# Unit 3's keys and values ahead of the last quarter of W2, and new early orders on four engines

## The chip, the core and the metric

The kernel runs on one core of one Trainium2 chip. Its engines are TensorE (PE, matmuls; PEld is its weight load), VectorE (DVE), ScalarE (ACT), GpSimd (POOL) and SyncE (SP). They work from instruction streams of their own and wait for one another on semaphores. The metric is the device time of one execution in microseconds, as the median of several runs. The kernel before takes 292.14 us (three runs, 292.03 to 292.19).

## What is computed

A linear attention with softmaxes over q's features and over k's sequence, then a feed-forward layer with an ELU:

```python
q_s = softmax(q, axis=-1)                    # 8 batches, 8 heads, 576 tokens, 64 features
k_s = softmax(k, axis=2)                     # over the 576 tokens
kv  = einsum('bhsd,bhse->bhde', k_s, v)
x   = einsum('bhsd,bhde->bhse', q_s, kv)     # -> 4608 tokens x 512
h   = x @ w_in                               # 512 -> 2048
g   = where(h > 0, h, exp(min(h, 0)) - 1)
out = g @ w_out                              # 2048 -> 512
```

## The kernel before, in words

**Units and blocks.** The attention runs in 16 *units*, four heads of one batch each (two units per batch). For unit n, `stage1` takes the exponentials of q and k on ScalarE, casts v to bf16 (tile `VB`), reduces q over features and takes the reciprocal on VectorE (`ZQ`, `RZQ`), and multiplies (`QS`) on VectorE or GpSimd. `tp` transposes `QS` on TensorE and copies it into `qsT`; from unit 4 on a transposing DMA on SyncE's queue (`turn`, tile `QT`) and a widening copy (`widen`) do it. `kv_mm` forms k^T v in PSUM, `m` divides by k's sums into `MBLK`, `ao_mm` (or `ao_parts` for units 0 and 1) multiplies `MBLK` with `qsT` into attention tokens, and `xt` copies them into the ring `XT`. A unit's nine chunks of tokens come in two pieces, so `ao` and `xt` run twice.

The feed-forward part runs in 9 *blocks* of 512 tokens. In each, 8 *groups* g of 256 columns of W1 are multiplied with `XT` (`hg_mm`, four steps kc over the 512 features, two column tiles: 8 matmuls, line 620), then the ELU follows in `hg` (exponential at line 646, relu at 648, and a GR step at 652 or 659, that writes `GR` from PSUM and so empties two banks). Blocks 0 and 1 multiply `GR` with W2 in `out_mm` (line 673, 512 columns, four matmuls for a quarter of W2). Blocks 2 to 8 use a form with fewer products on sums of GR and of W2's quarters (`pair`, line 806).

**PSUM.** Eight banks in four pairs: b0 and b1, b2 and b3 (called `D_`), b4 and b5 (`C`), b6 and b7 (`AB`). In blocks 0 and 1 the pairs are shared between groups, W2 accumulators (one bank for each of four token tiles, `ts`) and the units' small products. Units from 2 on use `AB`, and unit 3 uses `C` for its transpose and its first token piece.

**Loads.** SyncE issues q, k and v of units 0 and 1 in the first 4 us. GpSimd issues W1, first in four pieces of 384 KB (groups 0 to 2, one piece for each kc, the kc=0 piece only when k of unit 0 has landed), then groups 3, 4 and 5 singly (512 KB each) and 6 with 7 (1 MB), then W2 in four quarters of 1 MB (`load_w2`, resources `W2_0` to `W2_3`) mixed with the loads of units 2 and 3 (576 KB each). A transfer's landing is what its readers wait for.

**What sets the order.** The whole program is a list of about 1400 operations, each added with `Sched.add`, with the resources that it reads (R), writes (W) or holds (X). Dependencies follow from the order in which operations are added. The order on each engine is written out by hand in `ORDER`, as numbers in that list; where an operation may run on either of two engines (copies on ScalarE or VectorE, multiplies and casts on GpSimd, VectorE or ScalarE), its place in `ORDER` says which. `AFTER` adds four extra dependencies. Before unit 1's k^T v step (`spare_until`), spare matmuls fill TensorE's gaps as `Sched.fill` reckons them.

Block 0's order on TensorE: the small products of units 0 and 1; groups 0 to 2, kc by kc; groups 3, 4, 5, 7, 6; then the 16 steps of `out_mm` over four quarters of W2 (`jq`) and four token tiles, with the small products of units 2 and 3 between them; then block 1's groups.

## Time and profile before

| | |
|---|---|
| median of three runs | 292.14 us |
| span of the profiled execution | 290.4 us |
| TensorE busy | 280.6 us (97%) |
| VectorE busy | 225.5 us (78%) |
| ScalarE busy | 209.7 us (72%) |
| GpSimd busy | 167.8 us (58%) |
| TensorE's share of the chain that ended last | 94% |
| granted TensorE clock | 0.999 |
| moved by DMA | 50.04 MB, 172 GB/s over the span |

The page gives no time of the profiled execution other than its span, which runs from the first to the last instruction; the 1.7 us between it and the median lie around the span. Busy time of an engine counts its instructions without waits. A row of waits reads: who waited, for what, total us, number of times, longest. A row of the chain or of the timeline reads: start in us, length in us, engine, line, operation, tiles, count. A row of DMA issues ends with the size and the us from issue to landing. In the fences of the prediction, rows of one engine at one place come from the timeline of that stretch.

### The profile page before, as it was taken

The numbers are of one execution on the slowest core, as the hardware profiler recorded it, in microseconds if no ns is written. First come the engines' busy times: TensorE is split into PE (matmuls) and PEld (weight loads), VectorE is DVE, ScalarE is ACT, GpSimd is POOL, SyncE is SP. The second block draws the span as 40 slices with busy tenths as digits, with TensorE's granted clock in tenths as the row PEclk, the third lists the DMA queues.
The fourth block names the chain that finished last, engine by engine and source line by source line (L and its number), as shares of the span: only waits on it lengthen the run. The fifth ranks groups of instructions, "written<-read, shape, count | busy, mean of one in ns | idle before, by whom it ended". The sixth has DMA issues, their size and how long they took to land.

```text
span 290.4 us, 5465 instructions
## 1 busy us (share of the span) xinstructions
PE 280.6 (97%) x2176; PEld 243.7 (84%) x2176; DVE 225.5 (78%) x425; ACT 209.7 (72%) x237; POOL 167.8 (58%) x161
## 2 busy tenths in 40 slices
PE   2899999999999999999999999999999999999995
PEld 0488787778888899989999988989999999988995
DVE  3758834777699978989996987688977786794884
ACT  4857839989899899968995598975385656665510
POOL 1991335523869778676574886757314234277741
PEclk9999999999999999999999999999999999999999
DMA  7999999798896838739939295313102002300334
GB/s 259 399 363 390 389 389 339 163 260 323 238 349 163 241 91 228 202 78 305 178 96 222 56 292 129 76 40 71 46 18 56 0 2 67 78 2 1 92 73 128
DMA packets 36474, 50.04 MB, mean 172 GB/s; under 512 B 16352, under 2 KB 18144, under 8 KB 36448
## 3 DMA queue, kind: packets, MB, share of 16 engines
q1 hardware_dynamic: 29680, 33.96, 43.7%
q0 software_dynamic: 6528, 15.47, 17.8%
q8 instruction: 17, 0.28, 0.5%
q10 hardware_dynamic: 240, 0.26, 0.3%
q14 instruction: 9, 0.07, 0.1%
HBM read 36.70 MB, written 9.44 MB: 159 GB/s over the span
## 4 chain that ended last, share of the span: by engine, by line
PE 94%; DMA 2%; POOL 2%; SPq 0%; issue 0%; DVE 0%
PE PS L620 46%; PE PS L806 32%; PE PS L673 10%; PE PS L538 3%; DMA KR<-in_k_dram 2%; PE PS L507 2%; POOL W L377 1%; POOL VB L277 0%; PE PS L457 0%; POOL QS L433 0%; SPq L359 0%; PE PS L550 0%; DVE OSB L815 0%
## 5 line engine op out<-in xcount | busy, mean ns | idle before, releaser
L620 PE MATMUL PS<-XT,W 128*128 128x512 f32 x576 | 142.0, 393 | 0.1
L620 PEld LDWEIGHTS PS<-XT,W 128*128 128x128 f32 x576 | 105.0, 188 | 21.2 <-DVE GR L659 0.5
L652 DVE SCALAR_TENSOR_TENSOR GR<-PS,GE 128x512 fp32r<-128x512 f32 x112 | 76.8, 686 | 18.7 <-ACT GE L648 16.7
L646 ACT ACTIVATE GE<-PS 128x1024 f32<-128x1024 f32 x56 | 57.4, 1025 | 40.0 <-PE PS L620 34.2
L757 POOL TENSOR_TENSOR GR<-GR 128x256 fp32r<-128x256 f32 (+1 forms) x48 | 47.2, 996 | 31.5 <-DVE SB L757 16.6
L648 ACT ACTIVATE GE<-GE 128x1024 f32<-128x1024 f32 x56 | 59.4, 1061 | 1.4
L806 PE MATMUL PS<-W,GR 128*128 128x256 f32 x336 | 53.7, 283 | 0.0
L806 PE MATMUL PS<-TB,GR 128*128 128x256 f32 x336 | 51.3, 283 | 0.0
L806 PEld LDWEIGHTS PS<-W,GR 128*128 128x128 f32 x336 | 47.6, 191 | 1.7
L806 PEld LDWEIGHTS PS<-TB,GR 128*128 128x128 f32 x336 | 45.7, 191 | 0.7
L433 POOL TENSOR_TENSOR QS<-QR,RZQ 128x1152 f16<-128x1152 f32 (+1 forms) x16 | 30.4, 1898 | 21.4 <-DVE RZQ L423 19.7
L815 DVE TENSOR_TENSOR OSB<-OSB,PS 128x256 f32<-128x256 f32 x84 | 34.7, 416 | 10.3 <-PE PS L806 9.2
L673 PE MATMUL PS<-W,GR 128*128 128x512 f32 x128 | 32.7, 396 | 0.0
L757 POOL TENSOR_TENSOR GR<-SB,GR 128x256 fp32r<-128x256 f32 (+1 forms) x18 | 17.3, 971 | 24.6 <-PE PS L806 12.7
L673 PEld LDWEIGHTS PS<-W,GR 128*128 128x128 f32 x128 | 23.3, 188 | 5.0 <-DMA W<-in_moe_w_out_dram 0.5
L757 POOL TENSOR_TENSOR SB<-GR 128x256 fp32r<-128x256 f32 (+1 forms) x20 | 19.2, 965 | 13.7 <-DVE GR L652 6.4
L421 DVE TENSOR_REDUCE ZQ<-QR 128x18 f32<-128x1152 f32 (+2 forms) x18 | 21.7, 1207 | 6.1 <-ACT QR L419 4.8
L757 DVE TENSOR_TENSOR GR<-GR 128x256 fp32r<-128x256 f32 (+1 forms) x36 | 21.3, 603 | 0.6 <-PE PS L806 0.6
L277 POOL CAST VB<-VR 128x1152 bf16<-128x1152 f32 (+1 forms) x11 | 11.9, 1084 | 13.1 <-DMA VR<-in_v_dram 13.1
L646 ACT ACTIVATE ESB<-PS 128x1024 f32<-128x1024 f32 x16 | 16.1, 1024 | 4.5 <-PE PS L620 3.4
L399 ACT ACTIVATE KR<-KR 128x1152 bf16<-128x1152 f32 x16 | 18.4, 1155 | 0.8 <-DMA KR<-in_k_dram 0.8
L277 ACT ACTIVATE XT<-PS 128x512 fp32r<-128x512 f32 (+6 forms) x23 | 13.6, 595 | 6.3 <-PE PS L538 3.2
(58 smaller groups left out, 271.4 us busy)
## 6 DMA issues: line engine op xcount, KB each, us to landing
out_dram<-OSB SPq DMA_DIRECT2D x61, 128.0 KB, 2.4
QR<-in_q_dram SPq DMA_DIRECT2D x12, 576.0 KB, 4.9
KR<-in_k_dram SPq DMA_DIRECT2D x12, 576.0 KB, 6.3
VR<-in_v_dram SPq DMA_DIRECT2D x12, 576.0 KB, 5.1
W<-in_moe_w_out_dram POOLq DMA_DIRECT2D x4, 1024.0 KB, 16.7
QR<-in_q_dram POOLq DMA_DIRECT2D x4, 576.0 KB, 12.1
VR<-in_v_dram POOLq DMA_DIRECT2D x4, 576.0 KB, 13.0
KR<-in_k_dram POOLq DMA_DIRECT2D x4, 576.0 KB, 11.1
```

What stands on the lines that cost most here:

```text
L277: return e.activation(dst, src, AF.Copy) if e is self.nc.scalar else e.tensor_copy(dst, src)
L399: S.add("act", t_act(1152, False), lambda e: e.activation(ek[:, :, :, :].rearrange("p h c d -> p (h c d)"), flat(k), AF.Exp), key - 2, X=[ ...
L421: S.add("dve", t_dve(m), lambda e, qp=qp, zp=zp: e.tensor_reduce(zp, qp, AX.X, ALU.add), key - 3, R=[f"qR{i}{x}" for x in xs], W=[f"ZQ{i}{ ...
L433: lambda e, qp=q[:, :, a:b, :], rz=rz, dst=qs[:, :, a:b, :]: e.tensor_tensor(dst, qp, rz, ALU.mult),
L620: last = e.matmul(P[:, t * 512:(t + 1) * 512], self.W1[:, kc, tt * 128:(tt + 1) * 128], self.XT[:, kc, rc:rc + BLK], start=(kc == 0), stop ...
L646: S.add("act", t_act(1024, True), lambda e: e.activation(ge, P, AF.Exp), key, W=own, X=banks)
L648: S.add("act", t_act(1024, False), lambda e: e.activation(ge, ge, AF.Relu, bias=1.0, scale=-1.0), key, X=own)
L652: S.add("dve", t_dve(512 if j else 1024), lambda e, u=u: e.scalar_tensor_tensor(*(x[:, :, u, :] if j else x for x in (gt, P)), 0.0, ge[:, ...
L673: last = e.matmul(dst, self.tile(jb, jj, ts), self.W2[:, jj, c0:c1], start=(jj == 0), stop=(jj == 15))
L757: lambda e: e.tensor_tensor(dst, a, b, op), key, R=R, W=W, X=X, after=after)
L806: last = e.matmul(dst, a[i][:, y_, :], b[i][:, y_, :], start=start and i == 0 and y_ == 0, stop=stop and i == len(grps) - 1 and y_ == z - ...
L815: S.add("dve", t_dve(256), lambda e: e.tensor_tensor(dst, a, b, ALU.add), key, R=R, W=W, X=X, after=after)
```

## The change

The loads. W1's groups 4 and 5 come in one transfer of 1 MB. W2's last quarter comes in two halves of 512 KB, added after k and v of unit 3 in place of before them. W2's resources are named by eighths, `W2_0` to `W2_7`, and block 0's `out_mm` steps of the last quarter (`jq == 3`) are added as two steps of two matmuls each. The list has four operations more by it (one load less, one more, four steps more), so nearly every number in `ORDER` and `AFTER` is shifted by four; the `AFTER` pairs are the same operations as before.

The banks. Unit 3's transpose and its first token piece use `AB` (b6 and b7) in place of `C`.

The spare matmuls. `spare_until` is set one line earlier and names the same operation.

The orders. Up to about operation 300, that is in the first 60 us, the orders on TensorE, ScalarE, VectorE and GpSimd are new; after that they are the old ones. SyncE's is the old one throughout. With the old numbers turned into words, the differences are these.

- TensorE, start: transposes of unit 0 (both halves), unit 0's k^T v, its two token matmuls (bank 5, then 4), unit 1's second transpose, its k^T v, its first transpose, then groups 0 to 2. Before, unit 1's first transpose came second. Group 0 takes kc=0 and kc=1, group 2 kc=0, then unit 1's two token matmuls; before, the three groups' kc=0 came first.
- TensorE, W2 of block 0: unit 2's transpose after two steps (before: five); its k^T v after six (before: after all eight of the first two quarters); its first token piece directly before the third quarter's first step, its second one step later (before: three); unit 3's transpose one step after that, no longer beside unit 2's k^T v; unit 3's k^T v after all steps of the third quarter; its first token piece after three half steps of the last quarter, its second after three more; the last W2 step (bank 1) after block 1's group 1 and before its group 0.
- ScalarE and VectorE: to VectorE go unit 0's second `qsT` copy, unit 0's leftover token copy, unit 2's `qsT` copy, two W2 output copies, a token copy of unit 3, and the query multiplies of units 1, 2 and 3 for their second halves (from GpSimd). To ScalarE go the second cast of v of unit 1 (from GpSimd) and a token copy of unit 3. To GpSimd go the first-half multiplies of units 1 and 2 and unit 4's widening copy. Unit 1's second exponential of q comes before its first, unit 2's exponential of q before group 0's of block 0, unit 5's reciprocal (`RZQ`) after the first GR step of block 1's group 3.
- GpSimd's issues: W1's kc=1 piece, the cast of v of unit 0, the kc=0 and kc=2 pieces, q of unit 2, a multiply, the kc=3 piece, group 3, groups 4 and 5, groups 6 and 7, W2's first and second quarters, k and v of unit 2, q of unit 3, W2's third quarter, k of unit 3, a multiply, v of unit 3, the first half of the last quarter, the cast of v of unit 2, the second half. Before: the four kc pieces in order (the cast between the second and the third), group 3, a multiply and a cast, group 4, group 5, groups 6 and 7, W2's first quarter, q of unit 2, the second quarter, q of unit 3, v and k of unit 2, W2's third and last quarters, k and v of unit 3.

```diff
-    def load_w2(self, s, key, after=()):
+    def load_w2(self, jj0, jj1, key):
         w = self.w_out.rearrange("(jj p) c -> p jj c", p=128)
-        sl = slice(s * 4, (s + 1) * 4)
+        sl = slice(jj0, jj1)
         self.S.add("gp", ISSUE["gp"], lambda e: e.dma_start(self.W2[:, sl, :], w[:, sl, :]), key,
-                   W=[f"W2_{s}"], dma=f"w2{s}", nbytes=1 << 20, after=after)
+                   W=[f"W2_{s}" for s in range(jj0 // 2, jj1 // 2)], dma=f"w2{jj0}", nbytes=jj1 - jj0 << 18)
...
-        for g0, g1 in ((3, 4), (4, 5), (5, 6), (6, 8)):
+        for g0, g1 in ((3, 4), (4, 6), (6, 8)):
             self.load_w1(g0, g1, range(4), -30)
...
         self.side(0, -3, self.kv_mm(1, 0))
-        kv1 = S.ops[-1]
+        S.spare_until = S.ops[-1]
         self.m(1, 0, -12)
-        S.spare_until = S.ops[-4]
...
-        self.load_w2(0, -29)
-        self.load_w2(1, -29)
+        self.load_w2(0, 4, -29)
+        self.load_w2(4, 8, -29)
         for n, t in ((2, "k"), (2, "v"), (3, "q")):
             self.load(n, t, -28)
-        self.load_w2(2, -27)
-        self.load_w2(3, -25)
+        self.load_w2(8, 12, -27)
         for t in "kv":
             self.load(3, t, -26)
+        for jj in (12, 14):
+            self.load_w2(jj, jj + 2, -25)
...
-            ps, eng = (C if x == 0 else AB, "both") if n == 3 else (AB, "act")
+            ps, eng = AB, "both" if n == 3 else "act"
...
-                return n, lambda: self.tp(n, C if n == 3 else AB, due(n) - 4, ("act",))
+                return n, lambda: self.tp(n, AB, due(n) - 4, ("act",))
...
             for ts in range(4):
-                self.out_mm(0, ts, (ts + 2) % 4, 4 * jq, 4 * jq + 4, key)
+                for jj in range(4 * jq, 4 * jq + 4, 2 if jq == 3 else 4):
+                    self.out_mm(0, ts, (ts + 2) % 4, jj, jj + (2 if jq == 3 else 4), key)
...
-AFTER = ((208, 196), (227, 255), (234, 268), (300, 281))
+AFTER = ((212, 200), (231, 259), (238, 272), (304, 285))
```

4 lines of the change are left out of this document (2 added, 2 removed), and 138 rows, old and new, of the table ORDER.

## The prediction

> **What bounds the kernel now.** I read the page's head and its chain first, then the busy time by stage, then TensorE's waits, then the chain in order of time.
>
> ```profile
> span 290.4 us, 5465 instructions
> ```
>
> The chain that ends last is nearly all TensorE. The stage from 60 us on, where the change edits nothing, in the table of busy time by stretch (length, PE, PEld, DVE, ACT, POOL, clock, DMA share, GB/s):
>
> ```profile
> 60.00:287.10 227.10, 227.04 (x1725) 204.00 (x1723) 187.62 (x363) 165.42 (x183) 135.99 (x120) 1.00 0.49 128
> ```
>
> TensorE is busy for 227.04 of 227.10 us at full clock. So a shift of TensorE at 60 us reaches the end one to one, and the change is worth what it does to TensorE's position before that. What TensorE loses there (weight-load waits, then the chain in order of time: start, length):
>
> ```profile
> PEld PS L620 <- DVE GR L659: 0.5, 1, 0.5
> PEld PS L673 <- DMA W<-in_moe_w_out_dram: 0.5, 1, 0.5
> PEld PS L620 <- DVE GR L652: 0.5, 1, 0.5
> ```
>
> ```profile
> 31.80 3.06 PE PS L673 x12
> ...
> 42.63 3.67 PE PS L673 x16
> ...
> 54.05 2.11 PE PS L620 x8
> ...
> 58.95 3.91 PE PS L620 x16
> ...
> 64.57 1.81 PE PS L620 x8
> ```
>
> Undisturbed, 8 matmuls take 1.81 us, so 12 take 2.72 and 16 take 3.62. The pieces at 31.80, 54.05 and 58.95 are too long by 0.34, 0.30 and 0.29 (the one at 42.63 is not): W2's second quarter landing, VectorE emptying banks 2 and 3, VectorE emptying banks 0 and 1. Together 0.93 us, which is about all that better early orders could remove after the dense stream has begun. Its beginning is the other place:
>
> ```profile
> 14.20 1.66 PE L620 MATMUL PS<-XT,W 128*128 128x512 f32 x6
> 15.70 0.62 PE L550 MATMUL PS<-qsT,MBLK 128*128 128x512 f32 x2
> 16.16 13.32 PE L620 MATMUL PS<-XT,W 128*128 128x512 f32 x58
> ```
>
> From 14.20 us on TensorE runs at 0.227 us a matmul. Group 3 of block 0 begins 18 matmuls after 16.16, at 20.24, and group 4 at 22.06.
>
> **The change, part by part.**
>
> *W1's first pieces change places.* GpSimd now issues the piece for kc=1 first and, behind the cast of v0, the one for kc=0, which TensorE needs first. Issue times and, of single issues, us to landing:
>
> ```profile
> 8.85 0.63 POOL L377 DMA_DIRECT2D W<-in_moe_w_in_dram  x1
> ```
>
> ```profile
> W<-in_moe_w_in_dram POOLq DMA_DIRECT2D x1, 384.0 KB, 5.5
> ```
>
> The second piece lands at 8.85 + 5.5 = 14.3 whichever it is, because the queue is behind (below), and the stream can begin at about 14.36 in place of 14.20: +0.16. Could the tokens be later than that?
>
> ```profile
> 11.68 0.61 DVE L520 TENSOR_TENSOR MBLK<-PS,RZK 64x128 fp32r<-64x128 f32 x2
> ```
>
> ```profile
> 13.73 0.68 DVE L277 CAST qsT<-PS 128x512 fp32r<-128x512 f16 x1
> ```
>
> ```profile
> 12.77 0.74 ACT L277 ACTIVATE VB<-VR 128x640 bf16<-128x640 f32 x1
> 13.40 0.60 ACT L277 ACTIVATE XT<-PS 128x512 fp32r<-128x512 f32 x1
> ```
>
> Unit 0's MBLK was ready at 11.68 + 0.61 = 12.29. It no longer stands behind a reduction and two reciprocals of unit 1 on VectorE, which gains 0.5 or so. VectorE then does a query multiply (0.7, priced as the 512-wide copy) and that qsT copy (0.68) that ScalarE did, so the token matmuls start at about 13.1 (estimate), the second ends near 13.6, and ScalarE's copy (0.60) at 14.2. ScalarE also takes v1's second cast from GpSimd, but sheds two copies ahead of it; had it shed nothing, the token copy would end at 13.51 + 0.74 + 0.60 = 14.85. I take +0.16; the ends are 0 and +0.65.
>
> *Unit 2's queries ahead of W1's kc=3 piece.* 576 KB at the 388 GB/s quoted below is 1.5 us, a 384 KB piece 1.0. The pieces land at 13.3, 14.3, 15.3, the queries at 16.8, kc=3 at 17.8. TensorE first used kc=3 six matmuls after 16.16, at 17.52; it would now come at 17.68 and wait until about 17.85. So +0.33 with the first term (ends +0.1 and +0.65).
>
> *Groups 4 and 5 of W1 in one transfer.* The old three issues and the first of W2:
>
> ```profile
> 13.56 2.28 POOL L377 DMA_DIRECT2D W<-in_moe_w_in_dram  x3
> 15.83 0.76 POOL L385 DMA_DIRECT2D W<-in_moe_w_out_dram  x1
> ```
>
> ```profile
> W<-in_moe_w_in_dram POOLq DMA_DIRECT2D x1, 512.0 KB, 5.7
> ```
>
> ```profile
> W<-in_moe_w_in_dram POOLq DMA_DIRECT2D x1, 512.0 KB, 6.4
> ```
>
> ```profile
> W<-in_moe_w_in_dram POOLq DMA_DIRECT2D x1, 1024.0 KB, 9.7
> W<-in_moe_w_out_dram POOLq DMA_DIRECT2D x1, 1024.0 KB, 11.7
> ```
>
> The issues start about 0.76 apart, at 13.56, 14.4 and 15.1. Group 4 landed at 13.56 + 5.7 = 19.3, group 5 at 14.4 + 6.4 = 20.8, groups 6 and 7 at 15.1 + 9.7 = 24.8, W2's first quarter at 15.83 + 11.7 = 27.5. So the same 1 MB took 4.0 us once and 2.7 the next time. In 20.8 to 22.1 us:
>
> ```profile
> DMA packets 239, 0.50 MB, mean 388 GB/s; under 512 B 0, under 2 KB 0, under 8 KB 238
> ...
> q8 instruction: 1, 0.02, 5.5%
> ```
>
> The engines moved 388 GB/s all along, 1.55 MB in 4.0 us, so nothing was idle: one 16 KB instruction packet held up one of the 16, and the transfer landed with its slowest, 1.3 us late. [...]
> The new sequence: kc=3 at 17.8, group 3 at 19.3 (512 KB took 1.5: 20.8 against 19.3), groups 4 and 5 at 22.0, or with the packet inside their transfer at 23.3. TensorE wants group 4 at 22.06 + 0.33 = 22.4; before, it had landed 2.8 us ahead of use. Ends 0 and +0.9; I take +0.85, because the packet's old place, moved with TensorE, falls inside 19.3 to 22.0.
> [...]
>
> *The three stalls.* W2's second quarter lands about 0.3 earlier (one transfer in 2.7 in place of two in 3.0) and is used after one more step, so 0.34 goes. Block 1's groups 0, 2 and 3 now come behind one W2 step (4 matmuls, 0.9 us) put after group 1's, and VectorE frees banks 2 and 3 in time: 0.30 goes. The last (0.29) depends on ScalarE and VectorE that follow TensorE closely; I take it as gone, it may stay. Sum −0.93, ends −0.6 and −1.0.
>
> *Unit 3 in banks 6 and 7; more pieces.* All of units 2 and 3 is one row of fill, copy, fill there. The second token matmul of unit 2 now has one W2 step (0.91) before it in place of two, against 0.71 for the copy and the hops: +0.05. A transpose and a k^T v step that stood together are parted: one more restart of 0.1. Sum +0.15 (0 to +0.3). W2's last quarter in halves adds waits at two places, not matmuls.
>
> *Queues.* On GpSimd k3 and v3 pass W2's last quarter, whose first half waits behind a multiply and whose second stands behind v2's cast. By the same steps (24.8 + 1.5 − 0.3, then 2.7 for 1 MB and 1.5 for a load) the halves land at about 43.0 and 44.3, and the queue is backed up till then, so late issue costs nothing. The quarter was first used near 42.5; one more W2 step and the shift put that at 43.8 at least. If that room of 0.8 is gone, TensorE waits for what is over. SyncE's order is the same. On ScalarE the exponential of unit 2's queries now lies ahead of group 0's, in a gap it has:
>
> ```profile
> 18.18 1.94 ACT L646 ACTIVATE ESB<-PS 128x1024 f32<-128x1024 f32 x2 [1.45 <-PE PS L620]
> ```
>
> It takes about 1.2 (priced by its 1152 elements from two 1024-wide ones in 1.94), the gap is 1.45 and ends 0.33 later, so it hides; with the queries over 0.4 later than 16.8 the excess delays group 0. Copies moved to VectorE:
>
> ```profile
> 40.00:50.00 10.00, 10.00 (x82) 7.82 (x81) 2.53 (x6) 8.01 (x12) 3.39 (x4) 1.00 0.99 354
> ```
>
> VectorE is busy 2.53 of 10 us there, so some 3.5 us more hide. Finer names for W2's parts and the spare-matmul line change nothing that is run later.
>
> **Sum**: +0.33 + 0.85 − 0.93 + 0.15 = +0.4 on a span of 290.4. The median, 292.14, lies 1.7 above that span, and I keep this: about 292.5.
>
> **The rivals.**
>
> *Faster: the merged piece is in time.* If the packet falls after 22.0, or on an engine that is ahead, +0.85 goes and −0.45 is left: 291.7, with all ends favourable 291.2. For it: there are 0.4 us of room without the packet. Against it: the packet came in that place before, and the room is a third of its delay. [...]
>
> *Slower: unit 5's turned queries come late.*
>
> ```profile
> 57.72 2.12 POOL L433 TENSOR_TENSOR QS<-QR,RZQ 128x1152 f16<-128x1152 f32 x1 [1.68 <-DVE ESB L657]
> ```
>
> ```profile
> QT<-QS SPq DMA_TRANSPOSE x1, 7.5
> ```
>
> ```profile
> 67.71 1.17 ACT L277 ACTIVATE qsT<-QT 128x1152 fp32r<-128x1152 f16 x1
> ...
> 69.22 0.51 PE L538 MATMUL PS<-qsT,MBLK 128*128 128x384 f32 x2
> ```
>
> The reciprocal ahead of this multiply is moved behind the GR step of block 1's group 3. That group's matmuls end near 56.2 (54.05 + 2.11); two ScalarE passes of 1.0 and a 0.7 step on VectorE follow, with ScalarE's queue between: 59 to 60, an estimate. So the multiply starts 1.5 to 2.4 us later; with 2.4 the transpose is issued at about 62.4. It took 7.5 us before and would then land at 69.9; copy and hops end at 71.1, where TensorE wants it at 69.6: +1.6, or 294.1. It decides from 5.9 us of transpose upward. For it: this very transpose was slow, and its margin was 0.3. Against it: the 12 of the trace have a median of 4.1.
>
> ```profile
> DMA to landing us min/median/max: 2.9/4.1/7.5
> ```
>
> *Slower: VectorE's new load* reaches a bank that TensorE waits for, one multiply (0.7) late: about 293.2. Against it: the idle time above.
>
> **How the numbers follow.** Within 0.2%, 0.6 us, is about what a measurement of this kernel can tell from no change. The forecast, a stall on the merged piece against three removed stalls, 0.45: 292.5, its own range 292.0 to 292.9. In time, 0.27. Late turn, 0.20. VectorE, 0.08. Faster: two thirds of the second case, 0.18. Slower: the late turn, most of VectorE and a fifth of the forecast, 0.34. Same: 0.48. Range 291.3 to 294.0: the second case nearly whole, the late turn up to its price.
>
> **What would show it.** The first W1,XT matmul at 14.3 to 14.4; a wait near 17.8 on W1; one of 0.5 to 0.9 at 22 to 23 on W1, the largest of TensorE's after the start; no wait on W2 at 31; chain pieces of 1.81 and 3.6 at 54 and 59. Wrong if group 4 starts by 22.5, if QT lands more than 5.9 us after its issue, or if a wait on VectorE stands between 30 and 55 us.

## The result, and the profile after

The changed kernel takes 295.69 us (median of four runs, 295.51 to 296.11) against 292.08 us for the kernel before on the same chip (four runs, 292.01 to 292.19): a ratio of 1.0124 with a 95% interval of 1.0109 to 1.0138. It is 3.6 us slower. The forecast was 292.5 us, with a range that ended at 294.0.

The profiled execution's span, and the stage from 63.5 us to 290.4 us in the table of busy time by stretch (length, PE, PEld, DVE, ACT, POOL, clock, DMA share, GB/s):

```profile
span 293.7 us, 5465 instructions
```

```profile
63.50:290.40 226.90, 226.90 (x1725) 203.82 (x1723) 187.28 (x361) 165.07 (x183) 137.98 (x121) 1.00 0.48 127
```

The span grew by 3.3 us, and in the late stage TensorE is busy all the time with the same 1725 matmuls as before. The loss lies ahead of 63 us. Among the waits of TensorE's weight loads (who, for what, total, times, longest), two name the places that matter here:

```profile
PEld PS L550 <- DVE qsT L277: 2.3, 1, 2.3
...
PEld PS L620 <- DVE GR L659: 1.0, 1, 1.0
```

No wait on W1 or W2 is among the longer ones, which is where the prediction had looked. The first place in the timeline of the changed kernel (start, length, engine, line, operation, tiles):

```profile
11.84 1.44 POOL L433 TENSOR_TENSOR QS<-QR,RZQ 128x640 f16<-128x640 f32 x1
11.86 1.98 DVE L433 TENSOR_TENSOR QS<-QR,RZQ 128x512 f16<-128x512 f32 x1
13.87 0.69 DVE L277 CAST qsT<-PS 128x512 fp32r<-128x512 f16 x1
14.62 1.22 PE L550 MATMUL PS<-qsT,MBLK 128*128 128x512 f32 x2 [1.41 <-DVE qsT L277]
...
17.34 2.02 PE L620 MATMUL PS<-XT,W 128*128 128x512 f32 x6
```

Unit 1's two query multiplies start 20 ns apart, GpSimd's first. VectorE's then takes 1.98 us, ending 0.56 after GpSimd's. Behind it on VectorE stands the copy of unit 0's turned queries, for which TensorE waits. Unit 0's token matmuls start at 14.62 in place of 12.35, W1's first matmul at 17.34 in place of 14.20. The six W1 matmuls there take 2.02 us, against 1.66 before. Groups by line in that stretch (busy us, mean ns of one), for the changed kernel at 12.6 to 18.3 us:

```profile
L457 PE MATMUL PS<-ID,QS 128*128 128x128 f16 x9 | 1.4, 312 | 0.0
...
L550 PE MATMUL PS<-qsT,MBLK 128*128 128x512 f32 x2 | 1.2, 714 | 1.4 <-DVE qsT L277 1.4
```

and for the kernel before at 12.3 to 18.3 us:

```profile
L550 PE MATMUL PS<-qsT,MBLK 128*128 128x512 f32 x4 | 1.4, 421 | 0.5 <-DVE MBLK L520 0.5
...
L457 PE MATMUL PS<-ID,QS 128*128 128x128 f16 x4 | 0.4, 222 | 0.2 <-POOL QS L433 0.2
```

The same shapes take 312 ns in place of 222 and 714 in place of 421: TensorE works slowly here, until about 18.3 us. The granted clock in the table by stretch does not say so, because the trace's list of granted clocks begins only at 18.18 us in this kernel, at full rate (in the kernel before at 9.99), and the table reads 1.00 where there is no entry:

```profile
14.60:18.30 3.70, 3.68 (x50) 2.77 (x51) 2.10 (x5) 1.28 (x2) 3.70 (x6) 1.00 1.30 378
```

The second place, in the chain in order of time and then in the timeline of the changed kernel:

```profile
53.60 1.83 PE PS L620 x8
...
59.56 1.53 DVE ESB L657
...
61.11 1.23 DVE GR L659
...
62.38 3.93 PE PS L620 x16
```

```profile
59.38 1.15 POOL L277 CAST qsT<-QT 128x1152 fp32r<-128x1152 f16 x1 [0.72 <-DMA QT<-QS]
59.56 1.51 DVE L657 TENSOR_SCALAR ESB<-ESB 128x1024 f32<-128x1024 f32 x1 [1.09 <-ACT ESB L646]
```

In the kernel before, the same VectorE operation stands in the timeline so:

```profile
56.94 0.69 DVE L657 TENSOR_SCALAR ESB<-ESB 128x1024 f32<-128x1024 f32 x1 [1.09 <-ACT ESB L646]
```

Beside GpSimd's widening copy of unit 4 (which was ScalarE's before) it takes 1.51 us in place of 0.69, and block 1's group 3 (the piece of 3.93 us) waits for what follows it. The piece at 53.60 is now 1.83 us long, so the stall for banks 2 and 3 is gone as forecast. In the prediction's chain it was 2.11.

How far TensorE is behind the kernel before at the same matmul, from the starts in the traces (us; the first two rows are absolute starts). The kernels of the other columns follow below.

| matmul | before | changed | GpSimd second | copy first | mended | mended, split | widening waits | queries behind | queries ahead |
|---|---|---|---|---|---|---|---|---|---|
| first token matmul | 12.35 | 14.62 | 13.33 | 12.55 | 11.40 | 11.63 | 11.89 | 12.40 | 12.37 |
| first W1 matmul | 14.20 | 17.34 | 15.53 | 15.28 | 14.18 | 14.41 | 14.68 | 15.50 | 14.54 |
| group 3, block 0 | 20.24 | +3.50 | +1.32 | +1.07 | +1.61 | +0.64 | +1.42 | +1.40 | +0.84 |
| after block 0's groups | 29.32 | +3.50 | +1.34 | +1.07 | +1.61 | +0.79 | +1.56 | +1.44 | +0.84 |
| group 3, block 1 | 58.95 | +3.44 | +1.26 | +0.98 | +1.51 | +0.79 | +0.71 | +1.39 | +0.16 |
| unit 4's first tokens | 62.69 | +3.46 | +1.31 | +1.00 | +1.50 | +0.82 | +0.67 | +1.36 | +0.20 |
| unit 5's first tokens | 69.22 | +3.46 | +1.30 | +1.00 | +1.50 | +0.82 | +0.67 | +1.36 | +0.96 |
| block 8 | 269.43 | +3.47 | +1.31 | +0.99 | +1.59 | +0.91 | +0.76 | +1.39 | +1.08 |
| **median time** | 292.08 | 295.69 | 293.62 | 293.36 | 293.33 | 293.74 | 292.91 | 292.62 | 292.64 |

All 3.5 us are lost before 20.24 us, and what lies between 29 and 63 us, where the prediction expected a gain of 0.78 (−0.93 + 0.15), comes to −0.04. So there are two questions: what the start costs, and what ate the gain.

### The profile page after: what moved, and what is told of

Read it like the earlier page. It is cut to its first block, busy times and chain, and to the rows that moved or that the text cites. A ratio compares the mean times of both kernels' runs of the same rounds, so it can differ in the third digit from the quotient of the medians.

```text
span 293.7 us, 5465 instructions
## 1 busy us (share of the span) xinstructions
PE 282.6 (96%) x2176; PEld 245.0 (83%) x2176; DVE 231.5 (79%) x431; ACT 207.3 (71%) x232; POOL 167.9 (57%) x160
## 4 chain that ended last, share of the span: by engine, by line
PE 92%; DMA 2%; DVE 2%; ACT 2%; SPq 0%; issue 0%
PE PS L620 44%; PE PS L806 32%; PE PS L673 10%; PE PS L538 3%; DMA VR<-in_v_dram 2%; PE PS L507 2%; PE PS L457 1%; ACT ESB L646 1%; DVE QS L433 1%; ACT KR L399 1%; PE PS L550 1%; DVE ESB L657 1%; SPq L359 0%; DVE GR L659 0%; ACT VB L277 0%
## 5 line engine op out<-in xcount | busy, mean ns | idle before, releaser
L433 POOL TENSOR_TENSOR QS<-QR,RZQ 128x1152 f16<-128x1152 f32 (+2 forms) x15 | 30.1, 2006 | 21.2 <-DVE RZQ L423 18.5
L277 POOL CAST VB<-VR 128x1152 bf16<-128x1152 f32 (+1 forms) x10 | 11.0, 1096 | 11.7 <-DMA VR<-in_v_dram 11.6
## 6 DMA issues: line engine op xcount, KB each, us to landing
KR<-in_k_dram POOLq DMA_DIRECT2D x4, 576.0 KB, 10.9
```

The costliest lines, as they stand in the source:

```text
L277: return e.activation(dst, src, AF.Copy) if e is self.nc.scalar else e.tensor_copy(dst, src)
L433: lambda e, qp=q[:, :, a:b, :], rz=rz, dst=qs[:, :, a:b, :]: e.tensor_tensor(dst, qp, rz, ALU.mult),
```

## The experiments

The theory after reading the two traces: (a) the two query multiplies, put side by side by the change, hold each other up; (b) TensorE, which waits for it, works at half its speed; (c) the gain of the later orders is eaten by the widening copy on GpSimd in the same way as in (a). Rivals: the order of the copy behind the multiply alone, the transfers, the W1 pieces, ScalarE's order at 55 us. Numbers in the diffs are places in the changed kernel's list: 43 and 47 are unit 1's two query multiplies (first and second half), 35 is the copy of unit 0's turned queries, 51 the transposes of 43's product, 67 unit 2's load of queries. Each time stands beside runs of the kernel before on the same chip, whose medians were 291.9 to 292.2. Nothing of the computation is left out in any kernel but spare matmuls in one, whose results are read by nobody.

### The two multiplies

GpSimd's multiply waits for VectorE's:

```diff
-AFTER = ((212, 200), (231, 259), (238, 272), (304, 285))
+AFTER = ((212, 200), (231, 259), (238, 272), (304, 285), (43, 47))
```

> The changed kernel with one wait more: GpSimd's multiply of unit 1's first half of queries starts only when VectorE's multiply of the second half has ended. Nothing else differs. Theory (the two multiplies hold each other up, and TensorE then works on at half its speed): VectorE's multiply goes from 1.98 us back to about 0.7, the copy of unit 0's turned queries ends at about 13.3 instead of 14.57, the token matmuls start at 13.4 instead of 14.62, and the time falls by 1.2 us to about 294.4 if TensorE stays slow until 18 us as in the changed kernel, or by up to 2.7 us to 293.0 if the shorter wait lets it keep its speed. Rival (VectorE's multiply is slow for another reason, the transfers that write SBUF for one): it still takes about 2 us and the time stays at 295.7 or grows, as GpSimd's multiply now ends later.

The copy goes ahead of the multiply on VectorE:

```diff
-    "dve": ... 48 49 50 47 35 58 ...
+    "dve": ... 48 49 50 35 47 58 ...
```

> The changed kernel with two neighbours on VectorE exchanged: the copy of unit 0's turned queries goes ahead of the multiply of unit 1's second half, so the two multiplies may still meet, but the token matmuls don't wait for it. Theory: the copy runs from 11.85 to 12.55 (a copy out of PSUM isn't held up by GpSimd), token matmuls start at 12.7 instead of 14.62, and the time falls by 1.9 us to 293.8 if TensorE stays slow, or by 3 us to about 292.7 if it is fast from 12.7 on. Rival (what costs is the later queries of unit 1, not the copy behind the multiply): the multiply of the second half still ends late, unit 1's tokens with it, and the time stays within 0.5 us of 295.7.

Measured: 293.62 us (ratio to before 1.005, 1.003 to 1.007) and 293.36 us (1.0051, 1.0037 to 1.0066). Timeline of the first:

```profile
11.86 0.69 DVE L435 TENSOR_TENSOR QS<-QR,RZQ 128x512 f16<-128x512 f32 x1
...
12.63 1.26 POOL L435 TENSOR_TENSOR QS<-QR,RZQ 128x640 f16<-128x640 f32 x1 [0.66 <-DVE QS L435]
13.33 1.22 PE L552 MATMUL PS<-qsT,MBLK 128*128 128x512 f32 x2
```

and of the second:

```profile
11.80 0.69 DVE L279 CAST qsT<-PS 128x512 fp32r<-128x512 f16 x1
12.00 1.44 POOL L435 TENSOR_TENSOR QS<-QR,RZQ 128x640 f16<-128x640 f32 x1
12.53 1.47 DVE L435 TENSOR_TENSOR QS<-QR,RZQ 128x512 f16<-128x512 f32 x1
12.55 0.73 PE L552 MATMUL PS<-qsT,MBLK 128*128 128x512 f32 x2 [0.69 <-DVE qsT L279]
```

With GpSimd second, VectorE's multiply takes 0.69, and the token matmuls come 1.29 earlier, as expected; that the transfers slow it is excluded, for up to there they are the same. With the copy first, the multiplies meet again, VectorE's ends 0.56 after GpSimd's again, and a copy that reads PSUM runs beside GpSimd in 0.69. In both meetings the multiply that starts second, VectorE's, by 20 ns in the changed kernel and by 0.53 us here, is the one that grows most: 1.98 and 1.47 us against 0.69, where GpSimd's takes 1.44 against 1.26. The two kernels gained 2.1 and 2.3 us, with token matmuls that come 1.29 and 2.07 us earlier. In the first the gain is larger than that, and the rest is TensorE's speed: its token matmuls still take 1.22 us, but from 14.9 us on it is fast, in place of 18.3 (unit 1's k^T v at line 509 takes 0.49 us here, and 0.71 at 16.22 in the changed kernel):

```profile
14.85 0.49 PE L509 MATMUL PS<-VB,KR 64*64 64x65 bf16 x36
15.27 0.45 PE L459 MATMUL PS<-ID,QS 128*128 128x128 f16 x5
```

Its granted clock is first listed at 14.70 us. In the second kernel the token matmuls take 0.73: in that execution TensorE was at full rate from 9.02 us on.

### TensorE's speed after a wait

Three more spare matmuls ahead of unit 0's token matmuls (56 is the first of them) in the changed kernel:

```diff
+                count += 3 * (o.idx == 56)
                 if count > 0:
```

> The changed kernel with three more spare matmuls (on the identity, into a bank that nobody reads) ahead of unit 0's token matmuls, so that TensorE is busy through most of the 1.4 us in which it waits for VectorE there; the collision of the two multiplies stays. Theory (TensorE works at half its speed until 18 us because it was idle at 13.2 to 14.6): its matmuls are fast soon after 14.6, W1's first matmul starts at about 16.2 instead of 17.34, the whole is 1 to 1.5 us faster, 294.2 to 294.7. Rival (the slow speed lasts as long in the changed kernel whether TensorE waits or not): within 0.3 us of 295.7, or slower by what the last spare matmul takes too long (up to 0.4).

Measured: 295.79 us (1.0107, 1.0072 to 1.0142): a miss. (Two of the five executions, with a mean granted clock of 0.999 and 1.0, took 293.70 and 294.71 us; the three at 0.992 to 0.994 took 295.79 to 296.44.) The timeline of TensorE in the profiled one, of the second sort, shows why:

```profile
10.85 1.90 PE L894 MATMUL PS<-ID 128*128 128x512 f16 x8
14.80 0.73 PE L553 MATMUL PS<-qsT,MBLK 128*128 128x512 f32 x2 [2.05 <-DVE qsT L280]
...
16.18 0.71 PE L460 MATMUL PS<-ID,QS 128*128 128x128 f16 x5
```

This time TensorE had come to full speed before the spare matmuls (granted from 9.16 us on). All eight took 1.90 us and were done at 12.75, so that the wait was 2.05 and not shorter. The token matmuls (0.73) are still fast, the five transposes at 16.18 are slow, and in the table by stretch the granted clock shows it:

```profile
15.90:19.30 3.40, 3.40 (x47) 2.82 (x36) 1.38 (x5) 0.97 (x2) 3.40 (x6) 0.51 1.21 344
```

The clock falls to half for 3.4 us soon after the wait (0.51 as the mean of this stretch). In the changed kernel's own profile TensorE had not yet been fast when the wait came (its five spare matmuls at 10.90 took 2.31 us, where all eight took 1.90 here), and the slow start lasted until 18.3; the record reads 1.00 there, as it does over the first spare matmuls of the kernel before (five in 2.32 us at 5.51, four in 1.04 at 10.82). The opposite test takes spare matmuls from the kernel before, where nothing else changes:

```diff
-                if count > 0:
+                if count > 0 and free < 8500.0:
```

> The kernel before with only its first seven spare matmuls: the one at 9.6 us and the four at 10.8 to 11.9 are left out (their results are read by nobody). Theory (TensorE falls to or stays at half its speed when it waits in the start): the matmuls of units 0 and 1 and the first of W1 show durations of 0.31 us for 128x128 and 0.56 to 0.71 us for 128x512 instead of 0.22 and 0.37 to 0.45, and the time rises by 0.5 to 1.5 us. Rival (the speed doesn't hang on the spare matmuls): durations and time as before, within 0.2 us.

Measured: 294.05 us against 292.06 (1.0062, 1.0044 to 1.008; the medians give 1.0068). The table by stretch, and TensorE's groups at 12.4 to 18.3 us:

```profile
7.98:11.40 3.42, 1.89 (x49) 0.96 (x46) 2.07 (x3) 3.36 (x6) 3.08 (x6) 1.00 1.07 396
11.40:12.50 1.10, 0.00 (x0) 0.00 (x0) 0.97 (x5) 1.10 (x3) 1.10 (x3) 0.50 1.23 399
12.50:18.22 5.72, 5.70 (x50) 4.24 (x51) 1.94 (x5) 1.74 (x4) 5.72 (x9) 0.50 1.50 374
```

```profile
L550 PE MATMUL PS<-qsT,MBLK 128*128 128x512 f32 x4 | 2.2, 647 | 1.6 <-DVE MBLK L520 1.6
...
L457 PE MATMUL PS<-ID,QS 128*128 128x128 f16 x4 | 0.7, 318 | 0.0
```

Without the last spare matmuls TensorE idles 1.60 us at 10.9 to 12.5, the clock is at half from 11.40 to 18.22, and the kernel loses 1.8 to 2.0 us although the `MBLK` that it waited for came only 0.18 later: its first token matmul is 0.18 late, and group 3 of block 0, some six microseconds of work on, 2.17. So (b) holds in this: idle time of TensorE in the start cost it its speed here (0.50 from 11.40 to 18.22).

The length of one wait is not the measure, though. The clock fell here 0.5 us after the wait of 1.60 began. The changes of the record lie at multiples of 3.41 us from its first entry, here one and three of them (7.98 to 11.40 and 18.22), in the kernel before 82 (9.99 to 289.88). Before the fall TensorE had been idle for about half of such a stretch or more, in one wait or several: it was busy 1.89 us of it here, 1.93 in the kernel with the queries behind (below), 1.36 in the one with three more spare matmuls. No limit can be read from that, for the kernel with the queries ahead kept its full rate after a stretch with 1.82:

```profile
8.23:11.64 3.41, 1.82 (x52) 1.12 (x49) 2.34 (x7) 2.89 (x4) 3.13 (x5) 1.00 1.07 396
11.64:15.05 3.41, 3.02 (x51) 1.58 (x49) 3.00 (x8) 3.07 (x5) 3.41 (x6) 1.00 1.20 400
```

The first entry lies at 7.98 us in the kernel with fewer spare matmuls, at 9.02 with the copy first, 9.16 with three more spare matmuls and 9.99 in the kernel before, but at 14.70 with GpSimd second and 18.18 in the changed kernel, so the same wait may or may not fill half of a stretch. Why the rate was kept after 1.82 and lost after 1.93, no run shows.

### The start as before, a try that failed

The orders of the start as in the kernel before, all else changed; in a second kernel W1's groups 4 and 5 split as well:

```diff
-    "pe": 34 32 36 56 55 53 59 51 78 81 80 63 64 79 82 84 ...
+    "pe": 34 51 32 36 55 56 53 59 80 78 79 63 64 82 81 84 ...
-    "dve": ... 29 25 30 45 26 41 27 42 46 48 49 50 47 35 58 ...
+    "dve": ... 29 30 25 41 26 42 43 27 45 46 48 49 50 58 ...
-    "gp": ... 31 15 23 14 16 67 43 17 18 19 20 68 69 ...
+    "gp": ... 31 14 15 23 16 17 18 47 39 19 20 68 67 69 ...
```

> The changed kernel with the orders of the start, up to the first 12 W1 matmuls, as the kernel before has them (GpSimd's loads, spare matmuls' end and the engines of the two multiplies and of the turned queries' copies too); the merged W1 piece, unit 3's keys and values ahead of W2's last quarter in two parts, unit 3 in banks 6 and 7 and all later orders stay as changed. Theory (the whole loss is made in the start): W1's first matmul at 14.2 as before, the loss of 3.5 us at 24 us gone but for a wait of about 0.75 us on the merged piece of W1 near 22.4, W2's second quarter in time, and the time 292.1 (292.08 + 0.75 for the piece + 0.15 for the five more matmuls - 0.9 for the stalls, + 0.3 as the banks' stall had grown in the changed kernel). Rival (the loss lies in the later orders as well): above 293.

> As the kernel with the start of before, and W1's groups 4 and 5 in two pieces again. Theory (the merged piece is late once the start is as fast as before): no wait on W1 at group 4, and 0.6 to 0.8 us less than the kernel with the start of before alone: about 291.4. Rival (the piece is hidden, or the wait only moves to group 5): within 0.2 us of it.

Measured: 305.31 and 305.70 us. Neither theory was tested. Moving GpSimd's loads back moved unit 2's queries behind W1, while ScalarE's order still had their exponential ahead of group 0's. From the timeline of the first:

```profile
28.78 1.16 ACT L397 ACTIVATE QR<-QR 128x1152 f32<-128x1152 f32 x1 [12.23 <-DMA QR<-in_q_dram]
...
33.24 8.97 PE L622 MATMUL PS<-XT,W 128*128 128x512 f32 x30 [11.18 <-DVE GR L661]
```

ScalarE stood 12.23 us before that exponential, and TensorE 11.18. W1's first matmul came at 14.03, so the start itself was as good as before. What it shows is how tightly a load's place and its reader's place belong together.

### The start mended by three moves

43 goes back to VectorE, into its idle time at 9.4 to 11.0 us; 35 ahead of it; 51 ahead of unit 0's token matmuls:

```diff
-    "pe": ... 36 56 55 53 59 51 78 ...
+    "pe": ... 36 51 56 55 53 59 78 ...
-    "dve": ... 46 48 49 50 47 35 58 ...
+    "dve": ... 46 35 43 48 49 50 47 58 ...
-    "gp": ... 16 67 43 17 ...
+    "gp": ... 16 67 17 ...
```

> The changed kernel with three edits of the start's order: GpSimd's multiply of unit 1's first half goes back to VectorE, into the 1.6 us that it idles at 9.4 to 11.0; the copy of unit 0's turned queries goes there too, ahead of it; TensorE's transposes of that multiply's product go ahead of unit 0's token matmuls, as in the kernel before. All loads and all later orders stay as changed. Theory (all of the loss is in VectorE's orders of the start): no multiply is longer than 0.85 us but where GpSimd's cast stands beside it, token matmuls at 11.9 to 12.4, W1's first matmul at about 14.5 (its piece lands at 14.4), 0.3 later than in the kernel before, and all later matmuls with it: 292.2 if the merged W1 piece lands near 22.3, up to 293.1 if it lands at 23.2. Rival (the later orders lose too): W1's first matmul at 14.5 but over 293.3.

The same with

```diff
-        for g0, g1 in ((3, 4), (4, 6), (6, 8)):
+        for g0, g1 in ((3, 4), (4, 5), (5, 6), (6, 8)):
```

> As the kernel with the mended start, and W1's groups 4 and 5 in two pieces again. Theory of the prediction (the merged piece is late at group 4): 0.5 to 0.9 us faster than with the merged piece, no wait on W1 at group 4. Rival (it lands in time, or its wait comes back at groups 6 and 7, whose piece lands at about 25.8): within 0.2 us.

Measured: 293.33 (1.005, 1.003 to 1.0071) and 293.74 us (1.0046, 1.0025 to 1.0067). The first W1 matmul is at 14.18 and 14.41, as before the change. TensorE's waits after 12 us, first merged, then split:

```profile
PE PS L622 <- DMA W<-in_moe_w_in_dram: 1.5, 2, 1.3
```

```profile
PE PS L622 <- DVE GR L661: 0.7, 1, 0.7
...
PE PS L622 <- DMA W<-in_moe_w_in_dram: 0.2, 1, 0.2
```

In the first, the wait of 1.3 is for W1's kc=3 piece, which landed at 18.95 (issue to landing 7.4 us), in the second that piece landed at 18.00. No wait for the merged piece was seen in the first, and splitting it gained nothing, so the rival fits; but the executions of the two spread over 2.5 and 2.9 us, and a gain of half a microsecond would not show in the times. The 0.7 on VectorE at 60 us is in both (0.6 in the first), and the table's row 58.95 is within 0.1 us of the row above it in all kernels so far: it does not hang on the start.

### The wait at 60 us

ScalarE's exponential of group 2 (259 here) ahead of that of unit 5's keys, on the mended and split kernel:

```diff
-    "act": ... 204 212 259 265 ...
+    "act": ... 204 259 212 265 ...
```

> As the kernel with the mended start and W1's split pieces, and on ScalarE the exp of W1's group 2 in the second block goes ahead of the exp of unit 5's keys. Theory (the wait of TensorE at 62 us, 0.6 long, is for a gelu that stands behind that exp on ScalarE): the wait goes, and the time falls by 0.6 us. Rival (VectorE's or another wait is next): less than 0.3 us.

Measured: 293.95 us (1.0054, 1.0034 to 1.0074), no gain: the rival holds. The exponential did not even come earlier. It now waits 0.97 us for VectorE's GR step, and starts at 57.54, where it started at 55.77 in the kernel with the old order; TensorE is 1.76 us later here too (61.50 against 59.74 at group 3). VectorE's operation behind it stood beside the widening copy again:

```profile
57.54 1.03 ACT L648 ACTIVATE ESB<-PS 128x1024 f32<-128x1024 f32 x1 [0.97 <-DVE GR L661]
```

```profile
58.49 1.15 POOL L279 CAST qsT<-QT 128x1152 fp32r<-128x1152 f16 x1 [0.40 <-DMA QT<-QS]
58.60 1.59 DVE L659 TENSOR_SCALAR ESB<-ESB 128x1024 f32<-128x1024 f32 x1 [1.09 <-ACT ESB L648]
```

So the copy itself: it waits for that operation, on the mended kernel.

```diff
-AFTER = ((212, 200), (231, 259), (238, 272), (304, 285))
+AFTER = ((212, 200), (231, 259), (238, 272), (304, 285), (214, 259))
```

> As the kernel with the mended start, and GpSimd's copy that widens unit 4's turned queries (1.15 us) waits for VectorE's operation on group 2 of the second block (the one on ESB that took 1.5 to 1.6 us in every kernel with the changed orders and 0.69 in the kernel before). Theory (that copy, which the change moved from ScalarE to GpSimd, holds up VectorE just as the query multiply did, and so keeps up TensorE's wait for banks 0 and 1): the operation takes 0.7 us, TensorE's wait of 0.6 us near 60 us goes, and what the later matmuls are behind those of the kernel before falls by about 0.6 us between 58 and 63 us; the time by as much, to 292.7. Rival (the wait is for ScalarE's or another work that stands before it): the place of the wait stays and less than 0.2 us is gained.

Measured: 292.91 us (1.0034, 1.0019 to 1.0048), 0.4 below the mended kernel, which the spread of the two alone would not show. The traces do. Timeline and chain:

```profile
57.60 0.69 DVE L659 TENSOR_SCALAR ESB<-ESB 128x1024 f32<-128x1024 f32 x1 [1.09 <-ACT ESB L648]
...
58.43 1.15 POOL L279 CAST qsT<-QT 128x1152 fp32r<-128x1152 f16 x1 [1.52 <-DVE ESB L659]
```

```profile
59.82 3.70 PE PS L622 x16
```

The operation takes 0.69 again, the piece at group 3 is 3.70 long in place of 3.93, with no wait of TensorE ahead of it, and between 29.32 and 62.69 us the kernel now gains 0.89 on the kernel before (+1.56 to +0.67), where the changed kernel gained 0.04. (c) holds. Of the two kernels below, which have this wait as well, the one with the queries ahead gains 0.64 there; the one with the queries behind gains 0.08, because it waits 0.6 us for VectorE in this stretch, in another place (31.9 us).

### Unit 2's queries and W1's kc=3 piece

The queries behind W1 and W2's first quarter again, with unit 2's work on ScalarE, VectorE and GpSimd where I took its old places to be (mended, split; numbers one higher); then with the widening copy waiting as well; then with groups 4 and 5 merged too:

```diff
-    "act": ... 66 115 91 94 95 97 101 102 105 112 113 110 ...
+    "act": ... 66 91 94 95 97 101 102 105 112 113 115 110 ...
-    "dve": ... 67 118 92 93 96 119 98 99 103 106 107 114 109 121 124 125 127 ...
+    "dve": ... 67 92 93 96 98 99 103 106 107 114 118 109 124 119 125 120 127 ...
-    "gp": ... 16 68 17 18 19 20 21 69 70 71 72 73 74 75 120 76 77 117 78 132 ...
+    "gp": ... 16 17 18 19 20 21 69 68 70 71 72 73 74 75 76 77 78 121 132 117 ...
```

> As the kernel with the mended start and W1's split pieces, and unit 2's queries are loaded behind W1 and the first quarter of W2 again, with their exp, sum, reciprocal and multiplies at the places that they have in the kernel before. Theory (what is left of the loss in the first 20 us is W1's kc=3 piece behind those queries, 0.5 to 1.5 us by the runs): the piece lands near 16.6, no wait on W1 near 18, matmuls from 20 us on within 0.3 us of those of the kernel before, time 292.6 or below. Rival (the piece is late by chance of the transfers, or unit 2's work is missed later on): no gain beyond 0.2 us, or a new wait near 33 us.

> Both of these together on the mended start with split pieces. Theory: the start and the unit 3 part as good as before, the waits on W2's second quarter and on the banks gone or nearly so: 291.5 to 292.1, at or a little below the kernel before. Rival (what the changed orders gain at one wait is lost at the next): 292.5 or more.

> The same with W1's groups 4 and 5 in one transfer as in the changed kernel. Theory of the prediction: now that nothing ahead of it is late, TensorE reaches group 4 near 22.2 and waits there for the merged piece: 0 when it lands at 21.5, up to 0.8 when it lands near 22.8. Rival (hidden in any case): within 0.2 us of the same kernel with the pieces split.

Measured: 299.1, 298.0 and 296.7 us (the last of three executions; a fourth took 300.5). All three fell to one fault of these orders: unit 2's multiply on VectorE (120) now stands behind two ELU steps, and the transposes of unit 2 wait for it, in the first for

```profile
PE PS L459 <- DVE QS L435: 3.0, 1, 3.0
```

The other two wait 4.1 and 3.4 us there. They show that the kc=3 piece is in time when the queries are behind it (no wait on W1), and nothing on the merged piece. Two cleaner kernels differ in the queries' place alone (with the exponential and the sum that read them). Both have the mended start, the waiting widening copy, W1's first pieces in the old order and

```diff
-        for g0, g1 in ((3, 4), (4, 6), (6, 8)):
+        for g0, g1 in ((3, 4), (4, 5), (5, 6), (7, 8), (6, 7)):
```

(numbers two higher), with the queries ahead of kc=3 (-) or behind it (+):

```diff
-    "act": ... 67 116 92 95 ...
+    "act": ... 67 92 116 95 ...
-    "dve": ... 68 119 93 94 97 ...
+    "dve": ... 68 93 94 119 97 ...
-    "gp": ... 16 69 17 18 ...
+    "gp": ... 16 17 69 18 ...
```

> On the changed kernel: the mended start, the widening copy that waits for VectorE, W1's groups in four pieces with group 7 ahead of group 6 (TensorE takes them in that order), W1's first two pieces in the order of the kernel before, and unit 2's queries loaded behind W1's kc=3 piece, with their exp behind that of group 0 and their sum behind group 0's gelu. Theory (with both collisions gone, the kc=3 piece in time and no piece of W1 late, the later orders keep the gain at W2's second quarter and at the banks): W1's first matmul at about 14, no wait on W1, matmuls from 63 us on up to 0.5 us ahead of those of the kernel before, 291.6 to 292.0. Rival (the orders of the start leave TensorE with waits in which it loses its speed, and by chance more than the kernel before): over 292.5, with executions that spread over 2 us.

> The same with unit 2's queries loaded ahead of W1's kc=3 piece, and their exp and sum ahead of group 0's, as in the changed kernel. Theory (the step costs a wait on the kc=3 piece): that piece lands at 17.9 to 18.9, a wait on W1 of 0.3 to 1.4 us near 18, and 0.3 to 1.4 us more than with the queries behind it. Rival (the piece is hidden): within 0.2 us.

Measured: 292.62 us (1.0025, 1.0011 to 1.0039) behind, 292.64 us (1.0016, 1.0003 to 1.003) ahead, so this step makes no difference that can be measured, and neither kernel beats the one before. In the profiled executions each loses in its own place: ahead, 0.6 us for the kc=3 piece, which landed at 18.16; behind, 0.6 us at 31.9 for VectorE's GR step, with unit 2's sum of queries (1.35 us at 22.50) now in the chain that leads to it. The executions with the queries behind fall in two groups: eight of 292.14 to 292.81 us with a mean granted clock of 0.998 or more, and four of 293.54 to 293.71 with 0.993 or 0.994. The profiled one is of the second group. Its table by stretch, and VectorE and GpSimd ahead of that in the timeline:

```profile
12.50:16.00 3.50, 3.50 (x46) 2.03 (x47) 2.29 (x5) 2.33 (x4) 3.50 (x6) 0.53 1.21 404
```

```profile
9.64 0.81 DVE L435 TENSOR_TENSOR QS<-QR,RZQ 128x640 f16<-128x640 f32 x1
```

```profile
9.65 1.27 POOL L279 CAST VB<-VR 128x512 bf16<-128x512 f32 x1
```

Here VectorE's multiply was 10 ns ahead, and GpSimd's cast took 1.27 us in place of the 0.61 that it takes in the changed kernel: the mended start had moved the collision to the other side. TensorE waited 1.27 us, and the clock was 0.53 for 3.5 us. The price of one such spell is about 1.2 us (293.6 against 292.4).

The profiled execution with the queries ahead (293.26 us) lost its early gain otherwise: +0.20 at unit 4's tokens, then +0.96 at unit 5's. Its waits, and the transposing DMA's times to landing (min, median, max), are

```profile
PE PS L540 <- ACT qsT L279: 0.5, 1, 0.5
```

```profile
DMA to landing us min/median/max: 3.0/4.1/6.9
```

Unit 5's transpose took the 6.9 us. The last run put three spare matmuls into the wait of 1.3 us (38 is unit 0's k^T v there):

```diff
+                count += 3 * (o.idx == 38)
                 if count > 0:
```

> As the kernel with unit 2's queries ahead of W1's kc=3 piece, with three more spare matmuls in TensorE's wait of 1.3 us (9.7 to 11.0) ahead of unit 0's keys and values. Theory (the executions above 292.6 are those in which TensorE falls to half its speed in its waits of the start): fewer of them, median 292.1 or below, level with the kernel before or up to 0.3 us under it. Rival (the spread comes from the transfers): median and spread unchanged, 292.6 with 292.0 to 293.5.

Measured: 292.47 us against 292.19 (1.0011, 0.9996 to 1.0025), twelve executions from 292.19 to 294.06. It can't be told from the kernel before, nor from the one without these spare matmuls, so neither theory is settled by it. What spreads the executions of these last kernels without a fall of the clock stays open.

## Why the prediction was wrong, point by point

**"W1's first pieces change places" is the step that failed.** Its +0.16, with ends 0 and +0.65, was measured as +3.14: W1's first matmul came at 17.34. The step had the right chain: VectorE does "a query multiply (0.7, priced as the 512-wide copy) and that qsT copy (0.68)" and the token matmuls follow. The multiply took 1.98, because GpSimd's multiply, which the same change had put beside it, started 20 ns earlier. I had priced a two-input operation by a copy out of PSUM and had not asked what stood on GpSimd at that moment. Alone it does take 0.69, so the price was right and the overlap was not. Token matmuls came at 14.62 in place of "about 13.1" (1.29 of it undone by letting GpSimd go second).

The same step also went from the tokens to W1 too fast. It let W1 follow ScalarE's token copy at 14.2 and left out TensorE's own small matmuls of unit 1 in between. In the kernel before, W1 begins 1.85 us after the first token matmul (12.35 and 14.20), so from 13.1 it would have begun at about 14.95 and not at 14.36, and the change puts one transpose more there. With GpSimd second the tokens came at 13.33, near the forecast, and W1 still only at 15.53; the 1.3 us that are left of the loss in that kernel lie here (0.5 of them in token matmuls that still ran at half rate, 1.22 us against 0.73). The part on the pieces was right: in the mended kernel kc=0 landed at 14.1 and W1 began at 14.18.

**No term was there for TensorE's speed.** "From 14.20 us on TensorE runs at 0.227 us a matmul" was carried over to the changed kernel. There it had not come to full rate before the wait, and the same matmuls took 1.4 to 1.7 times as long until 18.3 us. Between the first token matmul (2.27 late) and group 3 (3.50 late), 1.23 us were added, and letting GpSimd go second brought 1.29 at the first and 2.18 at the second, so some 0.9 of the loss is of this kind. The kernel before without its last spare matmuls loses 1.8 to 2.0 us in the same way.

**"The three stalls", −0.93.** W2's second quarter and banks 2 and 3 went as forecast. For banks 0 and 1 the prediction said "I take it as gone, it may stay". It grew, and ate what the two others had gained: the net from 29 to 63 us was −0.04 in place of −0.78 (−0.93 and the +0.15 of unit 3's pieces). The cause is a move that the list of the change named and the prediction did not cost, unit 4's widening copy on GpSimd. With that copy held back the net is −0.89. The sizes were about right, and the step lacked the second collision.

**"Unit 2's queries ahead of W1's kc=3 piece", +0.33 with the first term.** The piece landed at 17.9 as forecast (17.8), and nobody waited, since TensorE was 3 us late. In the mended kernels, split and merged, it landed at 18.0 and 18.95, and TensorE waited 0.2 and 1.3 us there, and 0.6 in the kernels with the widening wait and with the queries ahead. So the wait is real and of the forecast size or larger (0.17 without the first term), but putting the queries behind the piece cost as much elsewhere: the two kernels that differ only in this place take the same time.

**"Groups 4 and 5 of W1 in one transfer", +0.85.** The piece landed at 23.2, as forecast for the case with the instruction packet inside (23.3; 14.38 + 8.8):

```profile
W<-in_moe_w_in_dram POOLq DMA_DIRECT2D x1, 1024.0 KB, 8.8
```

TensorE wanted it at 25.56, so the term was 0. In the mended kernel TensorE came to group 4 at 23.67 (22.06 + 1.61), 0.5 behind the piece, and splitting it made no measurable difference. In the kernel with the copy first it landed at 22.2 (7.7 us), and there, too, one instruction packet moved while it was in flight. So the packet, to which the prediction put down 1.3 us, does not by itself decide the landing, and what does stays open, as does whether the piece would stop a TensorE that is on time, which no run reached. In the traces of the two kernels the last of a transfer's sixteen landings came 1.11 us after the others for this piece (23.16 after 22.05) and 1.32 for groups 6 and 7 before (24.81 after 23.49), and 0.10 to 0.12 for the W1 pieces that had landed ahead of the packet. That the packet moves with TensorE, on which the +0.85 was taken, no run shows: it came at 20.14 us in the changed kernel, after 115 matmuls, and at 20.88 in the kernel before, after 133, so it was 0.74 earlier with TensorE 3.5 late.

**How the misses add up.** At group 3 of block 0 the forecast was +0.33 and the measurement +3.50; the merged piece cost nothing in place of 0.85; the stage from 29 to 63 us gained 0.04 in place of 0.78. The last two misses nearly cancel (−0.85 and +0.74), which is luck, so that nearly the whole miss is the start's.

**The queues.** W2's halves landed at 42.8 and 44.1 (forecast 43.0 and 44.3), and nobody waited. **The late turn** did not happen in the changed kernel, whose three transposes between 55 and 75 us took 2.9 to 3.0 us; it happened once in an experiment, at 6.9 us, for 0.8 us (+0.20 to +0.96), a little above the 5.9 from which the prediction said it decides. **VectorE's new load**, the rival with 0.08, came nearest, "one multiply late", but the place was the start and not a bank, and the price was 0.7 where the start lost 3.5.

The signs that were named did their work: the wait at 22 to 23 on W1 was absent, and the first W1 matmul at 17.34 in place of 14.3 to 14.4 pointed to the start at once.

## What to carry to other kernels

Before moving an elementwise operation between VectorE and GpSimd, look at what the other of the two does at that time. In these runs an operation of VectorE with two SBUF inputs, or a one-input one like the TENSOR_SCALAR below, beside a GpSimd multiply or cast on SBUF cost the second to start the rest of the first's time but for 0.13 to 0.15 us (on VectorE 1.98 and 1.51 in place of 0.69, on GpSimd 1.27 in place of 0.61), and 10 or 20 ns decided which. Where such a pair can't be avoided, an explicit wait that lets the one on the critical path go first is cheap (2.1 us gained here by one, and by another 0.8 in the stage that it was meant for, 0.11 to 0.89). In the first 20 us of a kernel count TensorE's waits as well as its work, and add them up over some 3.4 us: where they came to about half of it or more, the next 3.4 us or more ran at half speed in three kernels here (0.50 to 0.53), which cost 1.2 to 2 us in two of them, and at full speed in a fourth.

## What the runs showed of the hardware

The one-input TENSOR_SCALAR on VectorE (128x1024 in SBUF, 0.69 us, against 1.22 for the TENSOR_TENSOR of the same size that follows it) was held up by a GpSimd copy as well: it took 1.51 us in the changed kernel, 1.49 in the mended one, 1.59 with ScalarE's new order and, in the chain, 1.52 with the copy first and 1.61 in the mended and split one. A copy from PSUM was not (0.69 beside GpSimd's multiply, in the kernel with the copy first). The engine that went first wasn't free of it: GpSimd's 640-wide multiply took 1.44 us beside VectorE's and 1.26 behind it.

The granted clock fell to half within 20 us of the kernel's begin in the profiled executions of four kernels: 0.50 at 11.40 to 18.22 us with fewer spare matmuls, 0.51 at 15.90 to 19.30 with three more of them, 0.53 and 0.55 at 12.50 to 16.00 with the queries behind and with ScalarE's new order. TensorE had been idle for 1.3 to 2 us ahead of it (waits of 1.60, 2.05 and 1.27; 1.52 of the 3.50 us from 9.00 on in the last), and the fall lasted 3.41 us or twice that. It depends on the execution whether it comes: the kernel with the queries behind came out at 292.4 with a mean clock of 0.998 or more and at 293.6 with 0.993 or 0.994. The slow matmuls of the changed kernel (312 and 714 ns until 18.3 us), before it had once been fast, are not in that record, which begins at 18.18.
